# Element 0's channel mixing takes its weights from the tile they are converted to; eight places for weight units

## The chip, the core and the metric

The kernel runs on one core of a Trainium2 chip. The metric is the time of one execution on the device, in microseconds (us). The core has engines that run side by side, each through its own list of instructions in order: PE (TensorE, matrix products; its weight loads are shown apart as PEld), DVE (VectorE), ACT (ScalarE), POOL (GpSimd) and SP, which in this kernel issues the DMA transfers. They meet through semaphores: an instruction that waits holds up all that stand behind it on its engine. SBUF is the memory that the engines work in, PSUM holds the results of PE, and DRAM is the large memory outside.

## The reference

Eight elements (b = 0 to 7) go through an attention block and then a mixer MLP. All results are 32-bit floats.

```python
q_n, k_n = rmsnorm(q, g_q), rmsnorm(k, g_k)           # q, k, v: 8 x 12 heads x 448 x 64
scores = q_n @ k_n^T / sqrt(64)
attn = softmax(scores)                                 # over the last axis
x = (attn @ v) put together as 8 x 448 x 768
h = relu(x^T @ w_tok1) @ w_tok2                        # token mixing: 448 -> 256 -> 448
u = x + h^T
out = u + relu(u @ w_ch1) @ w_ch2                      # channel mixing: 768 -> 1536 -> 768
```

The four weight matrices of the mixer come as 64-bit floats. The kernel turns them into 32-bit floats itself.

## The kernel before, in words

**Weights.** `weight_chunks` (L135) cuts the weights into 40 chunks: four of `w_tok1` and `w_tok2`, which stay in SBUF, and 36 "stages" of the channel mixing's weights, 18 of `w_ch1` and 18 of `w_ch2`. A stage is 128 rows by 4 blocks of 128 columns, the four quadrants (input half, output half) of one tile. `weight_items` (L265) makes one step of a pipeline for each chunk: load the raw 64-bit words (two DMAs, L180), five passes over 128 x 512 elements to make a 32-bit float (DVE L230, L231, L233, then ACT L241, then DVE L248, L262), and `store` (L194), which writes the converted stage to DRAM (`ws1`, `ws2`, `ws3`). The converted stage lies in a tile of `stage_pool`, which has three.

**Channel mixing.** Elements 1 to 7 use Strassen's scheme in Winograd's form: seven products instead of eight on halves of the matrices. It needs sums of the four quadrants. `sum_items` (L200) reads each stored stage back from DRAM (`raw<-ws`), makes the four sums with three POOL instructions (L210, L211, L213), and writes them to DRAM (`ws<-raw`). `moving_sums` (L659) makes the sums of the moving side for each element, in the tile `tu`: two on DVE, two on POOL. Products take their weights as "units" of 384 KB that `load_units` (L685) reads from DRAM into a ring of six places (`UNITS = 6`). A unit is loaded only when its group is stored, or for a sum's unit, when its group's sums are written.

Element 0 comes too early for that scheme and makes eight plain products: `ch1_first` (L726) and `ch2_first` (L740). They also take their weights as units from DRAM: 24 units, up to four ahead. `ch1_first` makes six matmuls (twelve instructions in the trace) into one PSUM tile `m_ps`, and then ACT writes the relu of it into `hb` (L736). `ch2_first` makes two times six, and then DVE adds the PSUM tile to `uT` (L756). `m_tile` has two PSUM tiles in turn.

**The order of the work.** It is written out by hand. `run` (L124) goes through a list of (cost, function) and each function issues its instructions on all engines. `merge` (L27) interleaves lists in proportion to the costs. While element b is in the mixer, the attention of element b + 1 runs between its products: `att_step` (L467) is one of four steps of two head pairs (scores `s_ps` L338, exponentials `e` ACT L342, products with v `o_ps` L412, sums of exponentials `es` on POOL for two and DVE for four, L380, row sums `d_ps` L392, division by them L441 to L458 into `uT`). The normalisation of q and k is done some pairs ahead: `square` (ACT, L1105 for the first twelve pairs), `reduce` (DVE, L1122), `roots` (a Newton iteration, on POOL for most of the first pairs), `scale` (DVE, L303). For the squares of the first eight pairs there are two buffers: `sq_1` for pairs 1 and 3, `sq` for the others, so a square waits until the reduce before it has read the buffer.

The attention of element 0 runs alone, merged with `weight_items(0, BEFORE)`, where BEFORE is 4 + 14: fourteen stages' pipeline steps. The rest of the conversions is merged with element 0's token and channel mixing.

**Into the mixer.** `trans_x` (L607) turns `uT` for the token mixing. For elements 1 to 7 a DVE transpose (L624) writes it into `xt`, a tile of `tu_pool`, which has one tile; then it goes through DRAM (`xs`) back into `x`. The tiles `tu` of `moving_sums` and `v45` (values of pairs 4 and 5, at the start) are of the same pool. `tok1` (L632) multiplies by `w_tok1` and leaves relu in one of two `h1` tiles, `tok2` (L643) multiplies by `w_tok2` (L646), and DVE adds to `uT` (L651). At the end `trans_y` (L861) turns the result and `send_y` writes it to the output.

Of the kernel before, what the change touches and what calls it, by code (L numbers as in the profile page):

```python
# [44 lines left out]
def whole(ctx, tc, shifted, pre, q, k, v, g_q, g_k, moe_w_tok1, moe_w_tok2, moe_w_ch1, moe_w_ch2, out):  # L45


    nc = tc.nc
# [26 lines left out]
    UNITS = 6  # L75
# [17 lines left out]
    stage_pool = pool("stage_pool", 3)  # L93
# [57 lines left out]
    def stage_list():  # L151

        l = [(moe_w_ch1, mp, 2 * mp + i, t) for mp in range(KF // 2) for i in range(2) for t in range(KC)]
        l += [(moe_w_ch2, 4, m, t) for t in range(KF) for m in range(2)]
        l += [(moe_w_ch2, 3, 2, t) for t in range(KF)]
        return l
# [37 lines left out]
    def store(j):  # L194


        nc.sync.dma_start(out=slots(j, 0, 4), in_=st.pop(("stage", j))[:])
        st["stored"] = j if j + 1 < len(stages) else j + 1

    def sum_items():  # L200


        def one(i):
            n = len(stages)
            if i < n:
                t = st["sum", i] = raw_tile()
                nc.sync.dma_start(out=eight(t)[:, 0:4], in_=slots(i, 0, 4))
            if 0 <= i - 2 < n:
                q = eight(st["sum", i - 2])
                nc.gpsimd.tensor_tensor(out=q[:, 6], in0=q[:, 1], in1=q[:, 0], op=ALU.subtract)  # L210
                nc.gpsimd.tensor_tensor(  # L211
                    out=q[:, 4:6], in0=q[:, 1:7:5], in1=q[:, 3:4].to_broadcast([P, 2, P]), op=ALU.add)
                nc.gpsimd.tensor_tensor(out=q[:, 7], in0=q[:, 2], in1=q[:, 5], op=ALU.subtract)  # L213
            if 0 <= i - 3 < n:
                nc.sync.dma_start(out=slots(i - 3, 4, 8), in_=eight(st.pop(("sum", i - 3)))[:, 4:8])
                st["summed"] = i - 3 if i - 3 < n - 1 else n
                load_units(st["at"])

        def eight(t):
            return t[:].rearrange("p n w -> p (n w)").bitcast(F32).rearrange("p (q n) -> p q n", q=NQ)  # L220
        return [(1.0, lambda i=i: one(i)) for i in range(len(stages) + 3)]
# [28 lines left out]

    def convert_last(i):
        rows, srcs, dst = chunks[i]
        n = columns(i)
        if dst is None:
            q = st["stage", i - len(first)] = stage_pool.tile([P, 4, P], F32, name="stage")
            dst = q[:].rearrange("p q n -> p (q n)")
# [375 lines left out]
    def tok1(b, jc, h):  # L632
        cs = slice(h * HC, (h + 1) * HC)
        if h == 0:
            st["h1", jc] = h1_pool.tile([P, C], F32, name="h1")
# [36 lines left out]
    def unit_list(b):  # L672
# [4 lines left out]
        if b == 0:  # L677
            l = [part(mp, q, flat(ws1[mp, q])) for mp in range(KF // 2) for o in range(2) for q in (o, 2 + o)]
            l += [part(4, q, flat(ws2[tg, q])) for o in range(2) for q in (o, 2 + o) for tg in range(2)]
            return l + [single(q) for o in range(2) for q in (o, 2 + o)]  # L680
# [4 lines left out]
    def load_units(u):  # L685


        while st["loaded"] < min(u + (UNITS - 2 if u < first_units else UNITS - 1), len(units)):
# [3 lines left out]
            ready = st.get("stored", 0) if i < first_units or plain else st.get("summed", 0)  # L692
            if ready < stage_end[group] and i > u:
                break
            st["unit", i] = unit_pool.tile([P, 3, 2, P], F32, name="unit")
# [30 lines left out]
    def ch1_first(mp, o, j):  # L726

        u = st["uT", 0]
        if j == 0:
            st["w"] = next_units(2)  # L730
        ps = m_tile()
        for t in range(2 * KC):
            nc.tensor.matmul(  # L733
                out=ps[:, 0:S], lhsT=st["w"][t // KC][:, t % KC, j, :], rhs=u[:, t, :],
                start=(t == 0), stop=(t == 2 * KC - 1))
        nc.scalar.activation(  # L736
            out=natural(o)[:, :, 2 * mp + j, :], in_=ps[:, 0:S].rearrange("p (i n) -> p i n", i=2),
            func=AF.Relu)

    def ch2_first(o, half, m):  # L740

        if half == 0:
            st["m", m] = m_tile()
        if m == 0:
            st["w"] = next_units(2)
        elif m == 2:
            st["w"] = next_unit()
        ps = st["m", m]
        for t in range(KF):
            w = st["w"][:, t // 2, t % 2, :] if m == 2 else st["w"][t // KC][:, t % KC, m, :]  # L750
            nc.tensor.matmul(  # L751
                out=ps[:, 0:S], lhsT=w, rhs=natural(half)[:, :, t, :],
                start=(half == 0 and t == 0), stop=(half == 1 and t == KF - 1))
        if half:
            u = st["uT", 0][:, o * KC + m, :]
            nc.vector.tensor_tensor(out=u, in0=u, in1=st.pop(("m", m))[:, 0:S], op=ALU.add)  # L756
# [115 lines left out]

    def sends(b, cs):
        return [(0.3, lambda cc=cc: send_y(b, cc, st.pop(("y", cc)))) for cc in cs]
# [9 lines left out]
    def middle_items(b):  # L884
# [6 lines left out]
        if b == 0:  # L891
            items += [(us(6, S), lambda mp=mp, o=o, j=j: ch1_first(mp, o, j))
                      for mp in range(KF // 2) for o in range(2) for j in range(2)]
            return items, [(us(6, S), lambda o=o, h=h, m=m: ch2_first(o, h, m))
                           for o in range(2) for h in range(2) for m in range(2)]
# [8 lines left out]
    def last_items(b, sums):  # L904

        single = [(us(6, HS), lambda i=i: ch2(b, 1, i, 0)) for i in range(7)]
        if b == 0:
            single = merge(
                [(us(6, S), lambda o=o, h=h: ch2_first(o, h, 2)) for o in range(2) for h in range(2)], sums)
        l = turns(b, [0, 1, KC, KC + 1], not in_next(b))  # L910
# [5 lines left out]
    stage_end = [max(j for j, s in enumerate(stages) if s[1] == g) + 1 for g in range(5)]  # L916
    units = [u for b in range(B) for u in unit_list(b)]
    st["loaded"] = st["at"] = 0
    first_units = len(unit_list(0))
# [4 lines left out]
    BEFORE = len(first) + 14  # L924
    then = len(first) + stage_end[4] + 4
# [22 lines left out]
    for p in range(2):  # L948
# [3 lines left out]
        turn_qk(p, 0)  # L952
    pre.reduce(2, st)
# [10 lines left out]
    left, sums = [], sum_items()  # L964
    for b in range(B):
        early, double = middle_items(b)
        if b == 0:
            begin = x_items(0, 1) + tok1_items(0, 0) + tok1_items(0, 1)
            early = merge(begin + early, weight_items(BEFORE, then)) + merge(
                double, weight_items(then, len(chunks) + 3) + sums[:6])  # L970
        else:

            if in_next(b - 1):
                y, z = sends(b - 1, [0, 1, KC, KC + 1]), left
                left = [y[0], y[1], z[0], y[2], z[1], y[3]]
            run(merge(tok1_items(b, 0), left[:2]))
            begin, early = merge(tok1_items(b, 1) + early[:3 * KC], left[2:]), early[3 * KC:]
            if b == 1:
                early, double = merge(begin + early, sums[12:33]), merge(double, sums[33:])
                begin = []  # L980
            early = begin + early + double
        lo = (b + AHEAD) * per + 1
# [3 lines left out]
        tail = 4  # L986
        early, last = early[:-tail], early[-tail:]
        if b + 1 < B:
            last = merge(last, x_items(b + 1, 1))
        run(merge(att, early) + last + last_items(b, sums[6:12]))  # L990
        left = turns(b, [2, KC + 2])
# [49 lines left out]

# [198 lines left out]
```

## Time and profile before

| what | value |
|---|---|
| median of 7 runs | 1358.83 us (1353.76 to 1359.68) |
| profiled execution, its own time | 1353.69 us |
| span of the profiled execution | 1351.9 us |
| mean granted clock of PE | 0.992 |
| PE idle in the span | 64.8 us (1351.9 less 1287.1 busy) |
| of it: before the first product | 14.7 us |
| 24 instructions of L733 (12 products of 128x448) | 9.22 us |
| one unit from DRAM, issue to landing (L696) | 4.0 us |
| one raw stage read back, issue to landing (L207) | 4.8 us |
| DVE busy, 40 to 60 us / 260 to 280 us | 18.91 / 2.85 of 20 us |

Times in the page are microseconds unless ns is written. "Busy" is the time in which an engine executes; the page's chain follows the work that ended last back to what released each step. `a<-b` means that tile a is written from b; the figure after `x` is the count; what stands in brackets is the idle time of the engine before the instruction and what ended it. L numbers are lines of the kernel before. PEclk is the granted clock of PE as a share of full speed. The profiled execution is one of the faster ones: 5.1 us below the median.

### The profile page before, as it was taken

The page shows a single profiled execution, that of the slowest core. Times are in us where ns is not written, and L with a number is a line of the kernel's source. Part 1 is how long each engine was busy: PE and PEld are TensorE (multiplying, and loading weights), DVE is VectorE, ACT ScalarE, POOL GpSimd, SP SyncE. Part 2 cuts the span into 40 slices and gives each one's busy share as a digit, 9 for nine tenths or more (in the row PEclk, how much of TensorE's full clock was granted, in tenths as well). Part 3 has the DMA queues.
Part 4 walks back from the last instruction along what each step waited for, and adds up shares of the span by engine and source line. Part 5 has one row for each costly group of instructions (what it writes and reads, how often), then busy time and mean ns, then how long its engine had stood idle before and what let it go on. Part 6 is the DMA issues. An engine that isn't in the chain of part 4 may idle for free.

```text
span 1351.9 us, 20152 instructions
## 1 busy us (share of the span) xinstructions
PE 1287.1 (95%) x7408; PEld 926.0 (68%) x7408; DVE 754.2 (56%) x1295; ACT 365.5 (27%) x734; POOL 366.6 (27%) x406
## 2 busy tenths in 40 slices
PE   4889999999998999999999999999999999999997
PEld 2344444447778577785778767795777967787996
DVE  6988898345663455635655265644556365543212
ACT  5554433023230233212331223302332033300100
POOL 1202201257562232202331123312322034211220
PEclk9989999999999999999999999999999999999999
DMA  9785878989989566694559764594666956476655
GB/s 199 193 243 152 238 189 222 250 196 255 258 219 255 99 165 158 145 240 98 142 137 208 165 148 131 132 249 95 167 158 139 243 111 158 124 180 136 184 172 115
DMA packets 508143, 238.83 MB, mean 177 GB/s; under 512 B 374084, under 2 KB 466628, under 8 KB 508036
## 3 DMA queue, kind: packets, MB, share of 16 engines
q1 hardware_dynamic: 494914, 235.61, 69.5%
q10 hardware_dynamic: 12994, 1.84, 0.8%
q8 instruction: 61, 1.00, 0.3%
q14 instruction: 46, 0.38, 0.1%
q0 software_dynamic: 128, 0.00, 0.0%
HBM read 197.85 MB, written 39.52 MB: 176 GB/s over the span
## 4 chain that ended last, share of the span: by engine, by line
PE 74%; DVE 13%; DMA 4%; SPq 2%; ACT 2%; issue 2%; POOL 1%; ACTq 0%; DVEq 0%; POOLq 0%
PE m_ps L827 23%; PE m_ps L770 19%; PE s_ps L338 7%; PE o_ps L412 7%; PE m_ps L638 6%; PE m_ps L733 4%; PE m_ps L751 4%; PE m_ps L646 3%; DMA unit<-ws 2%; DVE es L380 2%; DVE qk_t L303 2%; PE d_ps L392 1%; ACT e L342 1%; DVE uT L651 1%; DVE qkT L318 1%
## 5 line engine op out<-in xcount | busy, mean ns | idle before, releaser
L827 PE MATMUL m_ps<-hb,unit 128*128 128x224 f32 x1764 | 342.1, 355 | 6.1 <-DMA unit<-ws 6.0
L827 PEld LDWEIGHTS m_ps<-hb,unit 128*128 128x128 f32 x1764 | 332.9, 191 | 21.7 <-issue 15.8
L770 PE MATMUL m_ps<-tu,unit 128*128 128x224 f32 x1008 | 202.8, 356 | 4.3 <-DVE r L775 3.0
L770 PEld LDWEIGHTS m_ps<-tu,unit 128*128 128x128 f32 x1008 | 188.3, 190 | 23.3 <-DVE r L775 5.5
L342 ACT ACTIVATE e<-s_ps 128x448 f32<-128x448 f32 x336 | 156.9, 546 | 90.7 <-PE s_ps L338 90.1
L770 PE MATMUL m_ps<-uT,unit 128*128 128x224 f32 x756 | 154.9, 357 | 6.0 <-ACT r L791 3.1
L770 PEld LDWEIGHTS m_ps<-uT,unit 128*128 128x128 f32 x756 | 140.4, 190 | 22.6 <-DVE uT L651 7.0
L338 PE MATMUL s_ps<-qkT 64*64 64x448 f32 x1260 | 148.2, 550 | 2.1 <-ACT x L618 1.9
L412 PE MATMUL o_ps<-e,v 64*64 64x448 f32 x1316 | 149.4, 541 | 0.1
L836 POOL TENSOR_TENSOR uT<-uT,r 128x448 f32<-128x448 f32 (+1 forms) x56 | 51.8, 936 | 265.6 <-DVE r L836 148.0
L775 DVE TENSOR_TENSOR r<-m_ps,r 128x448 f32<-128x448 f32 x63 | 39.0, 619 | 123.9 <-PE m_ps L770 76.2
L836 DVE TENSOR_TENSOR uT<-uT,m_ps 128x448 f32<-128x448 f32 (+1 forms) x70 | 34.1, 503 | 127.4 <-PE m_ps L827 127.4
L380 DVE TENSOR_TENSOR es<-es,e 128x896 f32<-128x896 f32 x84 | 93.9, 1118 | 13.3 <-ACT e L342 10.2
L412 PEld LDWEIGHTS o_ps<-e,v 64*64 64x64 f32 x1316 | 49.7, 133 | 68.4 <-issue 63.6
L338 PEld LDWEIGHTS s_ps<-qkT 64*64 64x64 f32 x1260 | 44.2, 132 | 74.4 <-issue 59.7
L775 POOL TENSOR_TENSOR hb<-r,r 128x448 f32<-128x448 f32 x21 | 27.7, 1319 | 229.9 <-ACT r L791 177.9
L380 POOL TENSOR_TENSOR es<-e 128x896 f32<-128x896 f32 x21 | 44.3, 2111 | 164.4 <-ACT e L342 164.4
L638 PE MATMUL m_ps<-x,w_sb 112*128 112x384 f32 x256 | 88.5, 500 | 0.0
L646 PE MATMUL m_ps<-w_sb,h 128*128 128x448 f32 x192 | 78.1, 549 | 6.8 <-DVE uT L651 6.8
L321 ACT ACTIVATE qkT<-qkT,g_t 128x448 f32<-128x448 f32 x36 | 24.0, 668 | 218.1 <-DVE qkT L318 218.1
L1122 DVE TENSOR_REDUCE ms<-sq 128x28 f32<-128x896 f32 (+2 forms) x47 | 51.2, 1092 | 50.8 <-ACT sq L1108 47.8
L638 PEld LDWEIGHTS m_ps<-x,w_sb 112*128 112x128 f32 x256 | 49.0, 194 | 36.8 <-ACT e L342 4.9
(100 smaller groups left out, 1345.4 us busy)
## 6 DMA issues: line engine op xcount, KB each, us to landing
unit<-ws SPq DMA_DIRECT2D x318, 384.0 KB, 4.0
raw<-in_moe_w_ch_dram SPq DMA_DIRECT2D x72, 256.0 KB, 3.9
v<-in_v_dram SPq DMA_DIRECT2D x94, 112.0 KB, 3.7
xs<-xt SPq DMA_DIRECT2D x56, 168.0 KB, 4.4
x<-xs SPq DMA_DIRECT2D x14, 672.0 KB, 6.2
out_dram<-turned SPq DMA_DIRECT2D x168, 56.0 KB, 2.1
ws<-stage SPq DMA_DIRECT2D x36, 256.0 KB, 4.0
raw<-ws SPq DMA_DIRECT2D x36, 256.0 KB, 4.8
```

Of the source, the lines that this page charges most:

```text
L338: nc.tensor.matmul(out=pss[i][rows_of(i, a), 0:S], lhsT=qkT[h, 1, k * D:(k + 1) * D], rhs=qkT[h, 0, :], start=True, stop=True)
L342: nc.scalar.activation(out=e[:, i, :], in_=pss[i][:, 0:S], func=AF.Exp)
L380: eng.tensor_tensor(out=es[:], in0=(es if k > 1 else st["e", t, 0])[:], in1=st["e", t, k][:], op=ALU.add)
L412: nc.tensor.matmul(out=st["o", p][a * D:(a + 1) * D, 0:S], lhsT=vt[rows, k * D:(k + 1) * D], rhs=e[rows, :], **kw)
L638: nc.tensor.matmul(out=ps[:, 0:HC], lhsT=w1_sb[0:R, c, jc * P:(jc + 1) * P], rhs=st["x", b, h][0:R, :, c, :], start=(c == 0), stop=(c == N ...
L646: nc.tensor.matmul(out=ps[:, 0:S], lhsT=st["h1", jc][:, cc * P:(cc + 1) * P], rhs=w2_sb[:, jc].rearrange("p c r -> p (c r)"), start=(jc == ...
L733: nc.tensor.matmul(out=ps[:, 0:S], lhsT=st["w"][t // KC][:, t % KC, j, :], rhs=u[:, t, :], start=(t == 0), stop=(t == 2 * KC - 1))
L751: nc.tensor.matmul(out=ps[:, 0:S], lhsT=w, rhs=natural(half)[:, :, t, :], start=(half == 0 and t == 0), stop=(half == 1 and t == KF - 1))
L770: nc.tensor.matmul(out=ps[:, j * HS:(j + 1) * HS], lhsT=w[:, t, j, :], rhs=m, start=(t == 0), stop=(t == KC - 1))
L775: add = lambda e, o, x, y: e.tensor_tensor(out=o, in0=x, in1=y, op=ALU.add)
L827: nc.tensor.matmul(out=ps[:, j * HS:(j + 1) * HS], lhsT=st["w"](j, t), rhs=hb[:, HB[what], t, :], start=(t == 0), stop=(t == KF - 1))
L836: add = lambda e, o, x, y: e.tensor_tensor(out=o, in0=x, in1=y, op=ALU.add)
```

## The change

Element 0's `ch1_first` and `ch2_first` are replaced by `first_stage(n)`, one call for each of the 36 stages. It takes the converted stage from the tile where DVE wrote it and makes four products with it: two outputs (o = 0, 1) by two input halves, into both PSUM tiles. A group of three stages (layer 1) or six (layer 2) ends with two relus or two additions. The 24 unit loads of element 0 go away; the stores of the stages to DRAM stay, since the other elements read them.

A converted stage now has to live until its products are made. `stage_pool` goes; `stage_home` puts the stages into the ring of units (stages 0 to 7, 15 to 20, 23 to 35), which has eight places and holds no units until element 0 is through; into a tile of `tu_pool` (8 to 12, and again 21 and 22); and into the `h1` tiles (13, 14).

The order changes with it. Ten stages' steps instead of fourteen are merged with element 0's attention, five steps with its token mixing, and the remaining 23 stand at fixed places between the products. Layer 2 goes by output block m = 2, 0, 1, six stages each. The sums of the last six stages are made by POOL straight from SBUF during element 0's last products; of the other 30 stages three items are run in element 0, 25 in element 1's first part and five in its second, first layer 1's and then m = 0 and m = 2. Four POOL instructions of 128x128 make a stage's sums in place of three. A third buffer for squares, `sq_2`, serves pairs 5 and 7. Units of elements 1 to 7 are loaded up to seven ahead, from the end of element 0 on.

```diff
-    UNITS = 6
+    UNITS = 8
-    stage_pool = pool("stage_pool", 3)
...
         l = [(moe_w_ch1, mp, 2 * mp + i, t) for mp in range(KF // 2) for i in range(2) for t in range(KC)]
-        l += [(moe_w_ch2, 4, m, t) for t in range(KF) for m in range(2)]
-        l += [(moe_w_ch2, 3, 2, t) for t in range(KF)]
-        return l
+        return l + [(moe_w_ch2, 3 if m == 2 else 4, m, t) for m in (2, 0, 1) for t in range(KF)]
...
+        def make(a, q):
+            nc.gpsimd.tensor_tensor(out=q[:, 6], in0=a[:, 1], in1=a[:, 0], op=ALU.subtract)
+            nc.gpsimd.tensor_tensor(out=q[:, 4], in0=a[:, 1], in1=a[:, 3], op=ALU.add)
+            nc.gpsimd.tensor_tensor(out=q[:, 5], in0=q[:, 6], in1=a[:, 3], op=ALU.add)
+            nc.gpsimd.tensor_tensor(out=q[:, 7], in0=a[:, 2], in1=q[:, 5], op=ALU.subtract)
...
+        def direct(i):
+            if i < n:
+                st["sum", i] = raw_tile()
+                make(st["stage", i], eight(st["sum", i]))
+            if i > n - 6:
+                send(i - 1)
+        order = [*range(n - 18), *range(n - 12, n - 6), *range(n - 18, n - 12)]
...
+    def stage_home(j):
+        if j in (8, 21):
+            st["stages"] = tu_pool.tile([P, 4, KC, HS], F32, name="stages", tag="tu")
+        if 8 <= j < 13 or 21 <= j < 23:
+            o = (j - 8) % 13 * 4 * P
+            return st["stages"][:].rearrange("p a b n -> p (a b n)")[:, o:o + 4 * P]
+        if 13 <= j < 15:
+            return h1_pool.tile([P, C], F32, name="stage", tag="h1")[:, 0:4 * P]
+        t = unit_pool.tile([P, 3, 2, P], F32, name="stage", tag="unit")
+        return t[:].rearrange("p t i n -> p (t i n)")[:, 0:4 * P]
...
-        while st["loaded"] < min(u + (UNITS - 2 if u < first_units else UNITS - 1), len(units)):
+        while ("stage", len(stages) - 1) in st["used"] and st["loaded"] < min(u + UNITS - 1, len(units)):
...
+    def first_stage(n):
+        w, _, m, t = stages[n]
+        wide = w is moe_w_ch2
+        last = (KF if wide else KC) - 1
+        if t == 0:
+            st["m", 0], st["m", 1] = m_tile(), m_tile()
+        a, u = st.pop(("stage", n)), st["uT", 0]
+        for o in range(2):
+            ps = st["m", o][:, 0:S]
+            for half in range(2):
+                nc.tensor.matmul(
+                    out=ps, lhsT=a[:, o + 2 * half, :],
+                    rhs=natural(half)[:, :, t, :] if wide else u[:, half * KC + t, :],
+                    start=(t == 0 and half == 0), stop=(t == last and half == 1))
+            if t < last:
+                continue
+            if wide:
+                to = u[:, o * KC + m, :]
+                nc.vector.tensor_tensor(out=to, in0=to, in1=ps, op=ALU.add)
+            else:
+                nc.scalar.activation(
+                    out=natural(o)[:, :, m, :], in_=ps.rearrange("p (i n) -> p i n", i=2), func=AF.Relu)
...
+    def first_items(tok, prods):
+        convert = weight_items(BEFORE, len(chunks) + 3)
+        items = merge(tok, convert[:5])
+        n = len(stages) - 13
+        for j, it in enumerate(prods[:-6]):
+            items.append(it)
+            items += [(0.0, convert[5 + k][1]) for k in range(len(convert) - 5) if begins(k, n) == j]
+        return items, prods[-6:]
+    def begins(k, n):
+        return 2 + -(-k * 27 // (n - 1)) if k < n else 29
...
-    BEFORE = len(first) + 14
-    then = len(first) + stage_end[4] + 4
+    BEFORE = len(first) + 10
...
+    pre.summand(pre.sq_2)
...
-                early, double = merge(begin + early, sums[12:33]), merge(double, sums[33:])
+                early, double = merge(begin + early, sums[3:28]), merge(double, sums[28:])
...
+        if b == 0:
+            last = x_items(1, 1) + merge(
+                last, direct + sums[:3], turns(b, y_order(b)[:4], not in_next(b)))
...
+        if b == 0:
+            load_units(0)
...
-            sq = (self.sq_1 if p in (1, 3) else self.sq)[0:rows]
+            sq = (self.sq_1 if p in (1, 3) else self.sq_2 if p in (5, 7) else self.sq)[0:rows]
```

## The prediction

> **What bounds the kernel now.** I read the page's busy times first, then the list of what PE (TensorE) waits for, then 20 us windows of the first element, and last the timeline around single stalls.
>
> ```profile
> span 1351.9 us, 20152 instructions
> PE 1287.1 (95%) x7408; PEld 926.0 (68%) x7408; DVE 754.2 (56%) x1295; ACT 365.5 (27%) x734; POOL 366.6 (27%) x406
> ```
>
> PE is busy 95% of the span: 1351.9 - 1287.1 = 64.8 us is idle. The change leaves the count of matmuls as it is (element 0's 72 + 72 products of 128x448 become 36 chunks of four, 144 again; the trace has two instructions for each product), so only those 64.8 us, the clock, and new waits are in play. The waits of PE (times, longest):
>
> ```profile
> PE s_ps L338 <- ACT e L342: 8.8, 3, 5.1
> PE m_ps L646 <- DVE uT L651: 6.8, 6, 1.7
> PE m_ps L827 <- DMA unit<-ws: 6.0, 3, 4.7
> PE m_ps L751 <- DMA unit<-ws: 3.2, 1, 3.2
> ```
>
> Two kinds are touched: scores that wait for exponentials in the first attention (8.8), and products that wait for weight units from DRAM (6.0 and 3.2). The windows (PE, PEld, DVE, ACT and POOL busy, granted clock, DMA share, GB/s) place them:
>
> ```profile
> 20.00:40.00 20.00, 16.48 (x166) 7.91 (x164) 17.30 (x30) 12.66 (x24) 3.16 (x11) 1.00 0.96 222
> 40.00:60.00 20.00, 14.60 (x120) 5.70 (x112) 18.91 (x32) 10.75 (x20) 3.02 (x9) 0.91 0.61 165
> 140.00:160.00 20.00, 20.00 (x95) 8.85 (x94) 19.41 (x28) 9.44 (x17) 4.50 (x2) 1.00 0.79 232
> 160.00:180.00 20.00, 20.00 (x92) 9.97 (x94) 15.66 (x24) 7.24 (x15) 2.88 (x12) 1.00 0.51 159
> 200.00:220.00 20.00, 16.78 (x69) 7.63 (x68) 18.23 (x31) 6.95 (x16) 4.25 (x2) 1.00 0.91 274
> 400.00:420.00 20.00, 15.27 (x87) 12.60 (x84) 6.71 (x12) 1.99 (x4) 6.63 (x10) 0.91 1.02 240
> ```
>
> At 20 to 60 us DVE (VectorE) is full and PE is not. At 140 to 180 PE is full, with DVE at 88% beside it. At 200 and 400 PE waits for DMA. The timeline of the two long stalls:
>
> ```profile
> 53.50 1.23 DVE L1122 TENSOR_REDUCE ms<-sq 112x16 f32<-112x1040 f32 x1
> 54.76 1.06 ACT L1105 ACTIVATE sq<-qk_t 112x1024 f32<-112x1024 f32 x1 [6.93 <-DVE ms L1122]
> 56.34 1.82 ACT L342 ACTIVATE e<-s_ps 128x448 f32<-128x448 f32 x4
> 56.91 1.01 PE L338 MATMUL s_ps<-hb 64*64 64x448 f32 x2 [5.05 <-ACT e L342]
> ...
> 414.80 3.62 PE L827 MATMUL m_ps<-hb,unit 128*128 128x224 f32 x9 [4.73 <-DMA unit<-ws]
> ```
>
> The first: ACT's next square shares a buffer with the one that DVE is still to reduce, so ACT stands 6.93 us, and the exponentials queued behind it, which PE needs, stand too. One of DVE's conversions, for the prices below:
>
> ```profile
> 98.09 0.69 DVE L248 SCALAR_TENSOR_TENSOR raw<-raw,e_t 128x512 uint32<-128x512 uint32 x1
> 98.81 0.43 DVE L230 TENSOR_SCALAR e_t<-raw 128x512 uint32<-128x512 uint32 x1
> 99.27 0.69 DVE L231 SCALAR_TENSOR_TENSOR raw<-raw,e_t 128x512 f32<-128x512 uint32 x1
> 100.00 0.43 DVE L233 TENSOR_SCALAR e_t<-raw 128x512 uint32<-128x512 uint32 x1
> 100.34 0.68 DVE L262 SCALAR_TENSOR_TENSOR stage<-raw 128x512 f32<-128x512 f32 x1
> ```
>
> **1. First attention (separate squares buffer, 4 conversions fewer).** The next one starts at 100.95: 2.86 us of DVE each. Four leave this stage: 11.4 us where DVE holds 18.91 of 20. With their own buffer the squares of pairs 5 and 7 no longer wait for a reduce. PE's stalls are 3.50 us (27.39 to 30.89) and 5.05; after the second the clock of 56 to 60 us is 0.57, another 4 x 0.43 = 1.7: at most 10.3. What comes next late is the exponentials' own queue behind conversions on ACT (0.70 each): about 1 us at the first stall, 1.4 at the second. I take -7.5, ends -10.3 and -2 (-2: DVE's scaling of q and k, L303 1.22 each, is late at the same place). The memset for the new buffer costs POOL 0.165 (row of L1045): +0.2 at most. Idle times at 80 to 100 us (1.9, 2.3, 0.6) stay.
>
> **2. Element 0's unit loads gone (24 x 384 KB).** Products take weights where DVE wrote them. The 3.2 us stall goes: -3.2. A price in its place: every product now needs its own conversion. From tok2's end to the 23rd chunk I count 97 to 103 us of DVE work against 115 us of PE; conversions lead by 11 chunks at first and by 6 at the end. Hidden by that lead; without it, rival C.
>
> **3. The tile of stages 21 and 22.** They live in the `tu` tile, which `trans_x` needs next for `xt`. In DVE's order the three `xt` transposes stand before two conversions and two `es` additions, and before the additions (ch2, as L756) that empty the PSUM tiles for the next group. The transposes now wait for the last matmul of stage 22. PE then has only stage 23 to do before it needs those two PSUM tiles (stages 23, 24, 25 stand together, no attention between, and there are two tiles in all). DVE: 3 x 0.61 (L624) + 2.86 + 2 x 1.12 (L380) + 2.86 + 0.62 (L756) = 10.4; PE: stage 23 is four products at 0.76 (24 instructions of L733 in 9.22 us are 12 products) = 3.0. New stall: 7.4. By 56 to 60 us such a gap also costs 1.7 of clock: +9.1. Ends +7.4 (the 3.50 us stall showed a full clock) and +11 (DVE two more us late; by my count it arrives 3 us early). Before, this transpose waited for nothing. Nothing excludes a larger loss, and a gain is excluded, since the order on DVE is fixed.
>
> **4. PSUM handover.** Each chunk writes both PSUM tiles, so a group's reader (relu 0.54 on ACT, addition 0.62 on DVE) has two products, 1.5 us, before PE wants the tile back; before it had a whole product group, 4.5. Eight handovers, of which three have no attention between: +0.8, ends 0 and +3 (three times a stretched exponential pair of 1.0).
>
> **5. Element 1's units.** With 8 places, 7 units ahead instead of 5; the sums of the last six chunks are ready in element 0, and the order of the rest brings the m = 0 and 1 groups one item earlier in a list 25 long over some 125 us, 5 us. That covers the 4.73 and most of the second, 1.1; the clock of 400 to 420 is 0.91, 1.7 again. -5.5, ends -7.5 and 0 (POOL, 4 instructions of 0.46 a chunk in place of 0.46 + 0.73 + 0.46, makes 25 instead of 21 there, 51 us for 38).
>
> **6. Element 1's first sums.** Before, the first nine chunks' sums were sent in element 0; now three are made there, and product T2 of layer 1 needs six. It starts at 315.75. POOL's order puts the sixth after two `es` (to 290.00), two sums, one `tu` pair and two more sums: by the old times of these places it ends between 304 and 309.6. Store 3.55 (chain, ws<-raw), unit 4.0 (landing), two issues of 0.5 (SP's rows by the stall: 0.60, 0.37): 312.6 to 318.2, so 0 to 2.5 us late, more if the sixth's raw load is held in SP's queue behind the 16 output stores that stand ahead of it. The second and third groups by the same walk: 0 to 2, and 0 to 4. +2.5, ends 0 and +10. The additions of L775 on POOL stand behind more sums: +0.7, ends 0 and +2.
>
> A rule that speaks against part 5. Row first: L211 on POOL takes 727 ns in the median and 1459 at most, L231 on DVE 694 and 2476: some meet and wait. The Trainium skill ("SBUF — State Buffer", section "SBUF: two separate sides") says why: the pair of ports that DVE and GpSimd share is held for a whole instruction, and the other side stands still. By it, each of 36 more POOL instructions could hold DVE up by its length, some 16 us of DVE as an estimate; by the windows DVE is busy 11 to 17 of 20 there, and the sum would move by 1 at most.
>
> **Sum.** -7.5 + 0.2 - 3.2 + 9.1 + 0.8 - 5.5 + 2.5 + 0.7 = -2.9. The profiled execution took 1353.7 (1.8 around its span), 5.1 below the median of the runs and at their lowest, so I put the change on the median: 1358.8 - 2.9 = 1355.9.
>
> **Rivals.**
> A. Forecast: the terms near their values.
> B. Units of element 1 late: the six sums come after 307 us, and T2 waits 6, then 2 and 4: +12 for +2.5, net +6.6: 1365. For: SP's long queue there, POOL at 11 to 15 of 20 already. Against: 7 units of depth. It decides from about 5 us of lateness.
> C. DVE becomes the bound of element 0's products: the lead of six chunks is used up when `es` and scaling bunch (19.41 of 20 at 140). Price two or three conversions, 6 to 9: net +5, 1364.
> D. The squares' wait is not what holds PE: DVE's scaling takes its place and part 1 gives 2: net +2.6, 1361.5.
> E. All unit waits go and part 1 is worth its end: -10.3 - 3.2 - 7.5 + 9.1, the small terms at nothing: net -12, 1347.
>
> **How the numbers follow.** A 0.50, B 0.18, C 0.12, D 0.10, E 0.10. What a measurement can tell here is 0.2%, 2.7 us. A lies at -2.9 give or take 5: faster 0.28, same 0.15, slower 0.07. B and C are slower but for 0.05 same; D half same, half slower; E faster. Faster 0.38, same 0.25, slower 0.37. Likeliest alone: 1351 to 1361. The range leaves out the low end of E and B together with C: 1345 to 1368.
>
> **What would show it.** Right: no stall of 3 us or more at 27 to 57 us; no waits for units in element 0; one PE stall of about 7.4 us in layer 2 of element 0, on DVE's addition, with a DVE wait on PE at the `xt` transpose ahead of it; in element 1 at most 3 us on units in layer 1. Wrong: a stall there above 5 us (B), products waiting for conversions (C), or the stalls of the first attention still standing (D).

## The result, and the profile after

The changed kernel is slower: 1361.74 us in the median (1357.96 to 1364.35), the kernel before 1357.74 us (1350.19 to 1361.61). The ratio is 1.0031, with a 95% interval of 1.002 to 1.0043. That lies inside the forecast's range and on the other side of no change: 4.0 us slower where 2.9 us faster was forecast.

The profiled execution after took 1361.84 us, close to its median. The one of before, 1353.69 us, was 4.1 us below the larger median, so the two traces differ by 8.2 us of span, about twice what the medians do. The sections below are differences between these two traces, so about 4 us of what they add up to belong to the fast execution of before, in which section is not known.

The page's head and the list of PE's waits of the changed kernel (in total, times, longest):

```profile
span 1360.1 us, 20152 instructions
PE 1291.8 (95%) x7408; PEld 930.5 (68%) x7408; DVE 748.2 (55%) x1295; ACT 365.6 (27%) x734; POOL 374.8 (28%) x443
```

```profile
PE m_ps L765 <- DVE uT L773: 7.2, 1, 7.2
...
PE o_ps L443 <- DMA v<-in_v_dram: 5.2, 2, 3.8
...
PE m_ps L848 <- DMA unit<-ws: 3.4, 1, 3.4
...
PE m_ps L848 <- DVE r L796: 2.3, 1, 2.3
...
PE s_ps L369 <- ACT e L373: 0.7, 2, 0.4
...
PE m_ps L791 <- DMA unit<-ws: 0.3, 1, 0.3
```

The scores' wait for exponentials (8.8 before) is down to 0.7, with 3.2 on transposes beside it; element 0's unit wait is gone. New are 7.2 us on DVE's addition (L773, in `first_stage`) and 5.2 us on the loads of v. To see where the time lies, I cut both spans at the first product of each element's token mixing (L638 before, L669 after). Four sections of the span:

| section | before | after | difference |
|---|---|---|---|
| start and element 0's attention | 99.1 | 92.4 | -6.7 |
| element 0's mixer, beside the attention of element 1 | 176.8 | 180.1 | +3.4 |
| element 1's mixer, beside the attention of element 2 | 166.9 | 180.1 | +13.2 |
| the rest | 909.1 | 907.4 | -1.6 |

The loss is in element 1, whose products the change does not touch. Windows over the two mixers (PE, PEld, DVE, ACT, POOL busy, granted clock, DMA share, GB/s), first of before, then of after:

```profile
99.12:275.88 176.76, 171.84 (x737) 80.88 (x737) 130.87 (x205) 54.27 (x103) 34.82 (x57) 0.99 0.78 211
275.88:442.83 166.95, 157.50 (x922) 118.75 (x920) 93.36 (x152) 42.11 (x87) 89.59 (x113) 0.99 0.93 236
```

```profile
92.42:272.55 180.13, 172.40 (x738) 81.26 (x738) 136.83 (x220) 57.25 (x106) 32.41 (x54) 0.97 0.60 154
272.55:452.66 180.11, 164.66 (x922) 122.15 (x921) 89.66 (x152) 41.88 (x87) 102.22 (x152) 0.96 0.93 237
```

In element 1 the DMA share is 0.93 and the rate 236 or 237 GB/s in both kernels, but there are 236 x 166.95 us = 39.4 MB before and 237 x 180.11 us = 42.7 MB after. In element 0's mixer it is the other way: 37.3 MB at a share of 0.78, then 27.7 MB at 0.60. Which transfers make up element 1's 3.3 MB, the counts of issues in the same two windows tell (size of each, median us from issue to landing), first of before, then of after:

```profile
unit<-ws SPq DMA_DIRECT2D x43, 384.0 KB, 5.1
ws<-raw SPq DMA_DIRECT2D x28, 256.0 KB, 4.2
raw<-ws SPq DMA_DIRECT2D x25, 256.0 KB, 4.5
```

```profile
unit<-ws SPq DMA_DIRECT2D x48, 384.0 KB, 5.6
ws<-raw SPq DMA_DIRECT2D x30, 256.0 KB, 4.3
raw<-ws SPq DMA_DIRECT2D x28, 256.0 KB, 4.6
```

Nine of the twelve sum items that ran in element 0 were moved to element 1, but six items are gone, since six stages' sums are now made straight from SBUF. That leaves three reads and two stores more, and five units more: before, three of element 1's units were loaded ahead of its start, after none, and the other two are loaded ahead for element 2. Three reads, two stores and five units are 3.3 MB. In element 2 of the changed kernel, where the DMA share is 0.67, a unit lands after 4.0 us instead of 5.6.

PE's part of the 13.2 us is 6.0 us more idle time (15.4 for 9.4) and 7.2 us more busy time for the same products, at a clock of 0.96 for 0.99.

### The profile page after: what moved, and what is told of

Its sections match the earlier page's. It is cut to its first block, busy times and chain, and to the rows that moved or that the text cites. A ratio compares the mean times of both kernels' runs of the same rounds, so it can differ in the third digit from the quotient of the medians.

```text
span 1360.1 us, 20152 instructions
## 1 busy us (share of the span) xinstructions
PE 1291.8 (95%) x7408; PEld 930.5 (68%) x7408; DVE 748.2 (55%) x1295; ACT 365.6 (27%) x734; POOL 374.8 (28%) x443
## 4 chain that ended last, share of the span: by engine, by line
PE 77%; DVE 10%; DMA 5%; ACT 2%; POOL 2%; issue 2%; SPq 1%; DVEq 0%; ACTq 0%; POOLq 0%
PE m_ps L848 25%; PE m_ps L791 18%; PE m_ps L765 8%; PE o_ps L443 8%; PE s_ps L369 7%; PE m_ps L669 5%; PE m_ps L677 3%; DVE es L411 2%; DVE qk_t L334 1%; DMA raw<-ws 1%; PE d_ps L423 1%; DMA unit<-ws 1%; DMA v<-in_v_dram 1%; PE m_ps L423 1%; ACT e L373 1%
## 5 line engine op out<-in xcount | busy, mean ns | idle before, releaser
L443 PE MATMUL o_ps<-e,v 64*64 64x448 f32 x1316 | 154.0, 544 | 5.3 <-DMA v<-in_v_dram 5.2
L669 PE MATMUL m_ps<-x,w_sb 112*128 112x384 f32 x256 | 87.3, 495 | 0.0
L669 PEld LDWEIGHTS m_ps<-x,w_sb 112*128 112x128 f32 x256 | 48.6, 193 | 36.4 <-ACT e L373 4.2
```

Of the source, the lines that this page charges most:

```text
L443: nc.tensor.matmul(out=st["o", p][a * D:(a + 1) * D, 0:S], lhsT=vt[rows, k * D:(k + 1) * D], rhs=e[rows, :], **kw)
L669: nc.tensor.matmul(out=ps[:, 0:HC], lhsT=w1_sb[0:R, c, jc * P:(jc + 1) * P], rhs=st["x", b, h][0:R, :, c, :], start=(c == 0), stop=(c == N ...
```

## Experiments on the parts of the change

Ratios are to the kernel before, run beside each. L numbers are of the changed kernel, where nothing else is said. A profiled execution differs from its kernel's median by up to 4 us, so sections that differ by less are not read as different.

**Stages 21 and 22 out of the `tu` tile.**

```diff
-        if j in (8, 21):
+        if j == 8:
-        if 8 <= j < 13 or 21 <= j < 23:
+        if 8 <= j < 13:
-        if 13 <= j < 15:
+        if 13 <= j < 15 or 21 <= j < 23:
```

> Stages 21 and 22 lie in the two h1 tiles (free since the token mixing) instead of the tu tile, so that the xt transposes have nothing to wait for. If the stall of 7.2 us in layer 2 of element 0 comes from that tile, it goes, with the clock that it costs (0.90 and 0.76 in the two 10 us stretches after it, 2.4 to 3.4 us): element 0's last product ends 9 to 10 us earlier, and the ratio to the kernel before falls from 1.003 to about 0.996. Rival: element 1 is bound by its transfers and sums, and gives the gain back: element 0 ends earlier, element 1 takes as much longer, ratio 1.001 to 1.003. Second rival: DVE is behind anyway and the additions come late without the tile, the stall stays above 4 us.

Measured: 1357.51 us, ratio 1.0017 (1.0005 to 1.0029). The stall fell from 7.19 to 3.94 us, not to zero. Timeline of the changed kernel, then of this one:

```profile
221.02 1.70 DVE L655 STREAM_TRANSPOSE xt<-uT 128x448 f32<-128x448 f32 x3 [3.12 <-PE m_ps L765]
230.52 1.15 DVE L773 TENSOR_TENSOR uT<-uT,m_ps 128x448 f32<-128x448 f32 x2
231.19 8.09 PE L765 MATMUL m_ps<-hb,stage 128*128 128x448 f32 x16 [7.19 <-DVE uT L773]
```

```profile
219.25 1.66 DVE L655 STREAM_TRANSPOSE xt<-uT 128x448 f32<-128x448 f32 x3
228.71 1.15 DVE L773 TENSOR_TENSOR uT<-uT,m_ps 128x448 f32<-128x448 f32 x2
229.38 1.02 PE L765 MATMUL m_ps<-hb,stage 128*128 128x448 f32 x2 [3.94 <-DVE uT L773]
```

The tile makes DVE wait 3.12 us, and that part went: 7.19 - 3.94 = 3.25. The other 3.94 us come from the order on DVE alone: three transposes, two conversions and two `es` additions stand ahead of the addition that PE waits for, and DVE runs through them without a gap. Both rivals had a point: the stall stayed near 4 us, and element 1 stayed at 180.4.

**The sums back into element 0.**

```diff
-                last, direct + sums[:3], turns(...
+                last, direct + sums[:12], turns(...
-                early, double = merge(begin + early, sums[3:28]), ...
+                early, double = merge(begin + early, sums[12:28]), ...
```

> Twelve sum items run in element 0's last products, as before, and 16 in element 1's first part, instead of 3 and 25. Theory: element 1 takes 13 us longer than before because the sums of the first group are not there when it begins, its units are all asked for at once (five at 308.7 us), and loads of q, k and v stand behind them in SP's queue: with the sums moved back, element 1 takes 166 to 170 us instead of 180, no waits of PE for v, ratio to before 0.994 to 0.997. Rival: four POOL instructions per stage or the ring of eight make element 1 slow whatever the place of the sums: 177 us or more, ratio 1.001 to 1.004. Second rival: the nine items now held in element 0 delay its last products or element 1's x: element 0 longer by 3 to 6 us.

Measured: 1366.71 us, ratio 1.0085 (1.0069 to 1.0101), and element 1 185.9 us. None of the three expectations fits: PE's waits for v went as the theory said, but element 1 did not get shorter, and the first rival's "177 us or more" came with another ratio and another cause. One new wait is larger than what went. In the list of PE's waits, and in the chain of work ahead of it (start, us, what):

```profile
PE m_ps L677 <- ACT h L672: 20.3, 1, 20.3
```

```profile
299.87 2.89 SPq L613
302.80 3.00 DMA out_dram<-turned
305.93 0.65 DVE turned L884
306.57 0.98 DVE ms L1164
307.57 0.24 ACT half L1172
```

The twelve items stand at the end of element 0 in the program, but most of their transfers are issued after element 1 has begun: 28 reads, 30 stores and 48 units fall in its window, as many as in the changed kernel. So this edit did not move the transfers back. Element 0's output stores stand behind them in SP's list, DVE waits for a free output tile, ACT for DVE's reduce, and PE for the relu behind that. With both edits at once:

> Both edits. If the two losses are apart from each other, the gains add: 9 to 10 and 10 to 13 us off the changed kernel, ratio to before 0.987 to 0.990. If the first only moves the wait into element 1, it is that of the sums alone, 0.994 to 0.997.

Measured: 1360.9 us, ratio 1.0047 (1.0031 to 1.0062): better than the sums alone by 0.0038, and far from 0.987. The same wait is 20.7 us.

**The squares of pairs 5 and 7 back in the shared buffer.**

```diff
-            sq = (self.sq_1 if p in (1, 3) else self.sq_2 if p in (5, 7) else self.sq)[0:rows]
+            sq = (self.sq_1 if p in (1, 3) else self.sq)[0:rows]
```

> The squares of pairs 5 and 7 go back to the buffer of the others; the four conversions stay out of the first attention. If the wait of the square for the reduce is what made the two long stalls, they come back: token mixing begins 4 to 7 us later than at 92.6 us, ratio to before 1.006 to 1.008. Rival: the four conversions fewer made the gain, the squares wait for less and the stalls stay under 1.5 us together: ratio 1.003 to 1.004.

Measured: 1362.56 us, ratio 1.005 (1.0033 to 1.0067), which overlaps the changed kernel's and lies between the two expectations. Token mixing begins at 92.49 us (92.42 with the buffer). The wait for the reduce is back, and costs PE little:

```profile
50.40 1.06 ACT L1147 ACTIVATE sq<-qk_t 112x1024 f32<-112x1024 f32 x1 [4.38 <-DVE ms L1164]
51.97 1.82 ACT L373 ACTIVATE e<-s_ps 128x448 f32<-128x448 f32 x4
52.55 0.97 PE L369 MATMUL s_ps<-hb 64*64 64x448 f32 x4 [2.50 <-ACT e L373]
```

PE's stall there is 2.50 us; with the buffer it is 2.41. The earlier stall is 0.94 us for 0.43. So the gain of 6.7 us in the first attention does not need the buffer; what is left of the change in that stage is the four conversions fewer (with the order they give), which were not undone by themselves.

## Experiments that moved the wait

These took single suspects out of element 1.

**The sums' stores from POOL's list.**

```diff
-            nc.sync.dma_start(out=slots(i, 4, 8), in_=eight(...)[:, 4:8])
+            nc.gpsimd.dma_start(out=slots(i, 4, 8), in_=eight(...)[:, 4:8])
```

> The changed kernel, but the 36 stores of sums (ws<-raw) are issued from POOL's queue, right behind the POOL instruction that makes them, instead of from SP. Same bytes, same order of the sums. Queue theory: element 1 is slow because SP's list runs in order and the loads of v, q and k stand behind stores that wait for POOL (8.4 us of waits in SP's list in element 1) and behind their issues (25 of 0.5 us): element 1 falls from 180 us to 170 to 174, PE's waits for v from 5.2 to under 1, ratio to before 0.995 to 0.999. Transfer theory: the 16 DMA engines are the limit (92% busy in element 1), and nothing moves: 178 to 182 us, ratio 1.002 to 1.004.

Measured: 1369.23 us, ratio 1.0084 (1.0063 to 1.0105), slower than either theory; element 1 184.3 us, waits for v 9.3. It is not a clean test: each store takes POOL 0.77 us (27.7 in all), and SP's list now waits 26.2 us for the stores to land before it loads the units that read them.

**Five units ahead instead of seven; three POOL instructions instead of four; sums counted as written one item later.**

```diff
-        while (...) and st["loaded"] < min(u + UNITS - 1, len(units)):
+        while (...) and st["loaded"] < min(u + UNITS - 3, len(units)):
```

> The changed kernel with units asked for five ahead instead of seven, the ring still of eight. If the bursts of unit loads (five at 308.7 us, four at 339.1) are what delays the loads of v, element 1 falls to 173 to 177 us and the waits for v to under 2; ratio 1.000 to 1.002. If they are not, element 1 stays at 179 to 181, or unit waits grow by 2 to 4 us; ratio 1.003 to 1.006.

```diff
-                make(q, q)
+                ...the three tensor_tensor of the kernel before, in place
```

> The changed kernel with the three POOL instructions per stage of the kernel before (0.46, 0.73 and 0.46) for the 30 stages that are read back, instead of four of 0.46. If POOL's time is what makes element 1 late, 25 stages at 0.2 us less give 3 to 5 us: ratio 0.999 to 1.001. If not, within 1 us of the changed kernel: ratio 1.002 to 1.004.

```diff
-            st["summed"].add(i)
+            st["summed"].update(st["sent"])
+            st["sent"] = [i]
```

> The changed kernel, but a group's sums count as written one item after the last store instead of at once, which is how the kernel before counted. A unit load issued right behind the store of the sums that it reads waits in SP's list for that store's landing (7.8 us in five waits in element 1, 3.5 in the kernel before), and everything behind it waits too. If that is a good part of the loss: PE's waits for v fall from 5.2 to 1 to 3 us, element 1 from 180 to 174 to 177, ratio to before 0.999 to 1.001. If the loads only change places: 179 to 181 us, ratio 1.002 to 1.004.

Measured: 1360.21 us (1.0018; 1.0002 to 1.0035), 1360.68 us (1.0026; 1.0013 to 1.0038) and 1360.13 us (1.0021; 1.0008 to 1.0033). Each interval overlaps that of the changed kernel; none of the three is a large part of the loss. In their traces element 1 takes 177.2, 175.2 and 177.3 us, 3 to 5 us less than in the changed kernel's; traces of one kernel can differ by about as much. The waits change places: with the later count v costs 2.0 us and units 7.7.

**Nine sum items in element 0, beside its last six stages, with the h1 tiles; then the last two output transposes later; then both with the later count; then twelve items.**

```diff
-                last, direct + sums[:3], turns(...
+                last, direct[:1] + merge(direct[1:], sums[:9]), turns(...
```

> Stages 21 and 22 in the h1 tiles, and nine sum items in element 0, among the direct ones from the 30th product on, instead of three after them; 19 in element 1's first part. Theory: the first group's sums are then written before element 1 begins, its units come one by one, and nothing that element 1's beginning needs stands behind the reads, since they are issued 15 us earlier than in the kernel with twelve: element 1 167 to 172 us, no stall of 20 us at the token mixing, ratio 0.991 to 0.995. Rival: each sum item moved into element 0 costs its 2 to 3 us of SP's list there, whatever its place, and holds up the output of element 0 and so the tiles that DVE turns it into: a stall of 8 to 15 us at the token mixing, ratio 1.000 to 1.004.

Measured: 1357.35 us, ratio 0.9998 (0.9985 to 1.0011). The rival held: a stall of 14.9 us at the token mixing, in the same place as the 20.3 above.

```diff
-                left = [y[0], y[1], z[0], y[2], z[1], y[3]]
+                left = [y[0], y[1], z[0], y[2], z[1], y[3]] if b > 1 else y + z
```

(For element 1 the last two of these now follow its token mixing.)

> As the kernel with nine sum items in element 0, but the last two of element 0's six output transposes on DVE come after element 1's token mixing instead of inside it. The four tiles that they turn into are then free. If DVE's 28.6 us wait for the output's transfers is what stalls the token mixing (14.9 us of PE), the stall goes to under 2 us, and with the clock it costs element 1 falls from 177.6 to 160 to 164 us; ratio 0.986 to 0.990. Rival: SP's list is late as a whole, the next wait in it (q and k for the scores, or the units) takes over, and at least half of the 14.9 us comes back elsewhere: ratio 0.994 to 0.998.

Measured: 1356.2 us, ratio 0.9994 (0.9983 to 1.0006). The 14.9 us went, and most came back 30 us later, as the rival said:

```profile
331.95 2.52 PE L443 MATMUL o_ps<-e,v 64*64 64x448 f32 x4 [9.84 <-DMA v<-in_v_dram]
```

> The one before, and a group's sums count as written one item later. If the two waits are apart, 2 to 4 us less than without: ratio 0.984 to 0.988. If unit loads are now issued too late for their products, unit waits of 2 to 4 us come in layer 1 or 2 of element 1: ratio as without it or 0.002 higher.

> Twelve sum items in element 0 instead of nine, with both edits. If SP's list has room at the end of element 0, 1 to 3 us less than with nine, from fewer sums in element 1: 0.983 to 0.987. If the list is full there, the output's stores and x come later: 2 to 5 us more than with nine.

Measured: 1355.54 us (0.9992; 0.9982 to 1.0002) and 1357.98 us (1.0003; 0.999 to 1.0017): the later count gives nothing that can be told, twelve items no more than nine.

**v from ACT's list; output stores from ACT's list.**

```diff
-            nc.sync.dma_start(
+            (nc.scalar if 2 * NPAIR <= p < 3 * NPAIR else nc.sync).dma_start(
                 out=vt[rows_of(p, a)]...
```

> The changed kernel with the twelve loads of v of element 2's pairs issued from ACT's list instead of SP's; nothing else leaves SP. If v is late because its issue stands in SP's packed list (issues of 45 us in the 54 us after element 1's start), PE's waits for v go from 5.2 to under 0.5 us, and with the clock they cost (0.85 and 0.81 in the 20 us after the first, 3.4 us) element 1 falls from 180 to 172 to 175; ratio to before 0.998 to 1.000. If the transfers themselves are late (landing 5.9 us), the waits stay at 3 to 5: ratio 1.002 to 1.004.

Measured: 1369.6 us, ratio 1.0107 (1.0088 to 1.0125). The wait for v is gone, and the units are late instead:

```profile
PE m_ps L791 <- DMA unit<-ws: 12.4, 2, 6.4
...
PE o_ps L443 <- DMA v<-in_v_dram: 0.5, 1, 0.5
```

> Stages 21 and 22 in the h1 tiles, nine sum items in element 0, the two late output transposes after the token mixing, and v of element 2's pairs issued from ACT. The one long stall of that kernel in element 1 was 9.84 us on v, with a clock of 0.73 and 0.59 after it (6.8 us in 20). If SP's list is the reason, both go: element 1 from 176.3 to 159 to 164 us, ratio 0.987 to 0.991. If the whole flow of transfers is late, the next wait (scores on q and k, units) takes over at least half: 0.994 to 0.998.

```diff
-            (nc.sync if in_next(b) else nc.scalar).dma_start(
+            (nc.sync if b and in_next(b) else nc.scalar).dma_start(
                 out=dst[:, i:i + 32]...
```

> The same without the change to v; instead the 24 output stores of element 0 are issued from ACT, which takes 15 us of issues out of the 45 in SP's list. By the theory of the packed list: v is in time, element 1 160 to 166 us, ratio 0.987 to 0.992. Rival: ACT's exponentials stand behind the stores, which wait for DVE, and PE waits 5 us or more for exponentials: 0.995 to 1.000.

Measured: 1357.0 us (1.001; 0.9998 to 1.0022) and 1365.72 us (1.0078; 1.006 to 1.0097). In both the 9.84 us went and others came: 5.54 us on DVE and 4.67 on ACT in the first; 9.05 us on element 1's x and 5.85 on the scores' q and k in the second. Element 1 takes 180.0 and 187.0 us, where the theory that one packed list of issues is the cause gave 159 to 166. Whatever was taken out of SP's list, another wait came, and the transfers of element 1 stayed at 41.3 to 43.2 MB in all these kernels.

## Experiments on the transfers' work

**The kernel before, with the sums placed as in the change.**

```diff
-                double, weight_items(then, len(chunks) + 3) + sums[:6])
+                double, weight_items(then, len(chunks) + 3) + sums[:3])
-        run(merge(att, early) + last + last_items(b, sums[6:12]))
+        run(merge(att, early) + last + last_items(b, []))
-                early, double = merge(begin + early, sums[12:33]), ...
+                early, double = merge(begin + early, sums[3:33]), ...
```

> The kernel before, with one thing of the change: three sum items in element 0 instead of twelve, the other nine in element 1. In the kernel before the DMA engines are busy 155 us of element 1's 167 (share 0.93), in every kernel with the change 164 to 171 us of 175 to 187. Transfer theory: element 1 lasts as long as its transfers, and nine reads and nine stores of 256 KB more make it 10 to 18 us longer, whoever issues them: 177 to 185 us, ratio 1.005 to 1.010. Rival: it is the ring, which in the kernel before already holds units when element 1 begins: element 1 stays within 3 us of 167, ratio 0.999 to 1.002.

Measured: 1367.96 us, ratio 1.008 (1.006 to 1.0099). Element 1's mixer takes 183.9 us:

```profile
272.90:456.77 183.87, 161.41 (x921) 119.23 (x920) 93.60 (x152) 41.87 (x87) 106.07 (x134) 0.98 0.92 230
```

Nothing else of the change is in this kernel, and element 1 loses 16.9 us, with 230 x 183.87 us = 42.3 MB at the same rate. Here nothing is dropped: its element 1 has 32 reads, 35 stores and 44 units, against 25, 28 and 43. So sum items added to element 1 are enough for a loss of that size; it is more of them than the change adds, and fewer units. (The first group's sums' units also come later, and PE waits 2.3 us in layer 1 for units. This run doesn't part that lateness from the bytes.)

**The sums of the first stages straight from SBUF, in element 0.** This is the kernel with the h1 tiles; POOL makes the sums just ahead of the stage's products, into a part of `hb` that element 0's mixer doesn't use.

```diff
+        def early(i):
+            if i < 12:
+                o = HB["T2"] * size + i % 7 * 4 * P
+                d = st["sum", i] = flat[:, o:o + 4 * P].rearrange("p (q n) -> p q n", q=4)
+                ...four tensor_tensor on POOL, from st["stage", i] into d
+            if i:
+                st["summed"].add(i - 1)
+                nc.sync.dma_start(out=slots(i - 1, 4, 8), in_=st.pop(("sum", i - 1)))
...
-        order = [*range(n - 18), ...
+        order = [*range(12, n - 18), ...
...
         for j, it in enumerate(prods[:-6]):
+            items += soon[j:j + 1]
             items.append(it)
...
-                early, double = merge(begin + early, sums[3:28]), merge(double, sums[28:])
+                early, double = merge(begin + early, sums[3:16]), merge(double, sums[16:])
```

> The changed kernel with stages 21 and 22 in the h1 tiles, and the sums of the first twelve stages made by POOL straight from SBUF, each just ahead of its stage's products, into a part of hb that element 0 doesn't use, and stored then, where the DMA engines are busy 0.2 to 0.6. Element 1 reads back and stores 18 stages instead of 30. Transfer theory: 11 reads and 12 stores fewer in element 1 at 0.7 to 0.9 us of all engines each take 16 to 20 us out of 166: element 1 158 to 164 us, ratio 0.987 to 0.992. Rival: POOL's 48 additions beside DVE's conversions hold DVE up, and element 0's products wait for conversions: element 0 3 to 10 us longer, ratio 0.993 to 1.000.

Measured: 1350.81 us, ratio 0.9944 (0.9927 to 0.996): faster than both kernels. The windows of its two mixers:

```profile
92.58:281.39 188.81, 175.59 (x737) 81.78 (x737) 142.40 (x220) 57.49 (x106) 69.93 (x102) 0.96 0.65 164
281.39:442.36 160.97, 154.82 (x922) 116.95 (x920) 91.33 (x152) 41.79 (x87) 75.47 (x104) 1.00 0.89 223
```

Element 1 is 19.1 us shorter than with the change alone, at 223 x 160.97 us = 35.9 MB. Elements 2 to 5 take 157.6 us each, so it is 3.4 us above what they need. Here, too, two things changed at once: the bytes are fewer, and the first group's sums are written before element 1 begins. Two numbers speak for the bytes: in the changed kernel product T2 waited only 0.30 us for its units, and the kernel before, which also wrote the first group's sums before element 1, took 6.0 us longer with 39.4 MB. No run parts the two altogether. Element 0 is 10.7 us longer than in the kernel with only the h1 tiles (178.1), so the rival's price holds too, but by another path than it named, which the list of waits shows:

```profile
PE m_ps L783 <- DVE uT L791: 9.5, 1, 9.5
```

```profile
DVE e_t L266 <- DMA raw<-in_moe_w_ch_dram: 7.0, 3, 3.2
```

DVE's conversions wait 7.0 us for the raw weights, which they did not before. Those loads and the sums' stores are both SP's; which of the two, list or transfers, holds them was not tried.

> The same with the first eighteen stages, so that element 1 has twelve left. Transfer theory: element 1 is then at PE's own time, 157 to 161 us, 1 to 4 us less than with twelve; ratio 0.985 to 0.991. Rival as with twelve, 2 to 5 us more in element 0.

Measured: 1357.14 us, ratio 0.999 (0.9981 to 0.9999). Element 1 takes 159.7 us, as expected (the ratio of 0.985 to 0.991 was not reached), with 32.6 MB at a share of 0.83; element 0 takes 195.4, 6.6 us more than with twelve. Past twelve stages element 1 has little left to give.

The kernels side by side (us of the two mixers, MB in element 1 as rate x length):

| kernel | element 0 | element 1 | MB in element 1 | ratio |
|---|---|---|---|---|
| before | 176.8 | 166.9 | 39.4 | |
| before, sums moved | 175.8 | 183.9 | 42.3 | 1.008 |
| the change | 180.1 | 180.1 | 42.7 | 1.0031 |
| the change, h1 tiles | 178.1 | 180.4 | 42.4 | 1.0017 |
| and twelve stages' sums from SBUF | 188.8 | 161.0 | 35.9 | 0.9944 |
| and eighteen | 195.4 | 159.7 | 32.6 | 0.999 |

At the rate of the kernel before, 236 GB/s, 42.7 MB take 181 us (180.1 measured) and 42.3 MB 179 (183.9); 35.9 MB would take 152, less than the 157.6 us that elements 2 to 5 last (161.0 measured). So element 1 lasts about as long as the longer of its transfers and its products.

## Why the prediction was wrong

**Part 1, first attention: right in size, wrong in one cause.** -6.7 us to the first product of the token mixing, for -7.5. Both stalls shrank (3.50 to 0.43, 5.05 to 2.41). But the working gave the wait of the squares for the reduce as the reason that ACT's exponentials were late; with the shared buffer back the gain stayed. So the buffer was not the cause; that the four conversions were is likely by what is left, and not shown.

**Part 2, unit loads of element 0: right.** No wait for units or conversions in element 0's products; rival C did not happen.

**Part 3, the `tu` tile: right in size.** 7.19 us for 7.4, DVE's wait for PE 3.12 for "3 us early", and a clock of 0.82 in the 10 us after it, 1.8 us for 1.7. The chain was the one described, but the tile was less of it than the heading said: without the tile 3.94 us remain.

**Part 4, PSUM handover: nothing seen** in PE's list of waits for +0.8. Parts 2 to 4 together gave +6.7 for element 0, and its section grew by 3.4, which is within what the two traces can differ by.

**Parts 5 and 6, element 1: the step that failed.** They came to -5.5 + 2.5 + 0.7 = -2.3, and element 1 lost 13.2. The waits that they priced went the right way: product T2 waited 0.30 us for its units, inside "0 to 2.5", and unit waits in layer 2 fell from 5.8 us in element 1 to 3.4, a gain of 2.4 where part 5 had 5.5. What they left out is the work of the transfers. Part 5 counts 25 items for 21 and prices them as POOL time alone ("51 us for 38"); seven units ahead count only as a gain. The three reads, two stores and five units that came to element 1, 3.3 MB, have no term: they were put at nothing, without a reason. The windows shown in the prediction had a DMA share of 1.02 at 400 to 420 us, which was read only as PE waiting for DMA at that place. Over the whole of element 1 it was 0.93 already, and at 236 GB/s 3.3 MB are 14 us; 13.2 were measured. That sum items added to element 1 lengthen it, and taken out shorten it, the runs show (183.9 us for 166.9 in the kernel before, 161.0 for 180.4 in the kernel with the h1 tiles). That it is by their bytes and not also by the first sums' lateness is the likelier reading, not a separate result. Rival B, the one on the slow side, named late T2 units as its mechanism, and that was wrong as well.

**The base.** -2.9 was put on a median; the difference of medians is +4.0, that of the two traces +8.2, since the trace of before is one of its faster executions.

## What to carry to other kernels

When work is moved from one stage to another, add up its bytes as well as its instructions, and set them against the DMA share of the stage that receives it. In the kernel before, the same nine sum items lengthened element 1 by 16.9 us, at a share of 0.93, while their leaving shortened element 0, at a share of 0.78, by only 1.0. A wait that only changes its name when its cause is taken away (v, units, x, output tiles) is a sign that something behind all of them is full. And data that a stage still holds in SBUF need not be read back: making the first twelve stages' sums at once gave the fastest kernel here, though it cost element 0 10.7 us, and eighteen gave no more.

## What the runs showed that was not expected

An output store can hold up the products of the next element: with four tiles to turn the output into, DVE waited 28.6 to 34.6 us for their transfers and PE 14.9 to 20.7 us behind it. Taking the v loads from one list of issues to another made the kernel slower by 0.0076 of its time, though PE no longer waited for v. And a separate buffer that removed a plain wait of 4.38 us on ACT gave nothing that could be told from the noise.
